# Attention and two MLPs on one core: sums of the second MLP for two blocks at a time on VectorE, shared accumulators, pools that wait by tile

## The chip, the cores and the metric

The kernel runs on one core of one Trainium2 chip. The metric is the device time of one execution in microseconds (us). Before the change it is 1059.33 us, the median of three runs (1056.86 to 1059.69).

## The reference, cut to what matters

All arrays are float32. Attention over 4 batches, 8 heads, 576 positions and 64 columns a head gives a matrix of 2304 tokens by 512. Two MLPs follow; only the second is touched by the change.

```python
def reference(**kwargs):
    attn_out = _attn_ref(...)                      # 4 x 8 x 576 x 64
    x = attn_out.transpose(0, 2, 1, 3).reshape(2304, 512)
    x = _moe_ref(x=x, ...)                         # 512 -> 2048 -> 512, leaky relu
    return _moe2_ref(x=x, ...)

def _moe2_ref(x, w_in, w_out):                     # 512 -> 2048 -> 512
    h = x @ w_in
    r = np.maximum(h, 0.0)
    return ((r * r) @ w_out).astype(np.float32)
```

## The kernel before, in words

The program is written in program order, and a scheduler orders the instructions of each engine by a timeline that it simulates at build time: on each engine an instruction of a later line may be put ahead of one of an earlier line if its operands are there sooner on that timeline. On the chip each engine then keeps the order it was given. All loads and stores go through SyncE's queue (SP), in order as well.

Precision: every float32 operand of a matmul is split into a rounded high part and the rest (`split2`, lines 738 to 741: a cast on ScalarE, line 740, and a subtraction on VectorE, line 741). A product is then three matmuls (`TERMS`: high by high, high by low, low by high).

The first MLP (lines 512 to 722) goes through five chunks of tokens (512, 512, 512, 384, 384), each with 16 steps over the hidden width. Chunk outputs are evacuated to the tiles `xT` (lines 255 and 257) and stored to `xD` in DRAM (line 676), three pieces of 768 tokens. Beside its matmuls the first MLP also prepares the weights of the second (lines 108 to 162). In a step VectorE makes `tt` and `gg` (lines 565, 566) and the low parts of `gs` and `wi` (lines 571, 518).

The second MLP uses Strassen's scheme with seven products for each of its two matrix products, in three passes of 768 tokens (`NPASS`). `part1.close()` (line 727) ends the pools of the first part; the pools `xcp`, `m2` and `ps` (PSUM, eight banks) open in the memory that they leave.

- `load_x` (line 743) loads the pass's inputs in one transfer of 1536 KB into `xl` (line 745). `x_steps` makes the seven split inputs `xc1` to `xc7`: `put` is a split of 128 x 768 elements, `diff` a subtraction in place on GpSimd (line 760). There are seven puts and four diffs.
- `stage1`: for each of eight blocks `q` of the hidden width seven products of six matmuls (line 813), with weights loaded by `w1_group` (line 774, split into `w1h`). Sums of products are made on VectorE (lines 835 to 860); ScalarE applies the relu and GpSimd the square (lines 823, 824). The results of a block are the four parts of a tile `g`, 128 x 4 x 384, one tile for each block.
- `Stage2`: seven sums over the eight blocks in the order of `ORDER2` (products 1, 5, 6, 2, 7, 4, 3), 56 items in all, nine matmuls each (line 927). `prepare` runs `AHEAD` = 3 items ahead: for products 5, 6, 7 and 4 it first subtracts two parts of `g` in place on GpSimd (lines 885, 887, 889, 891), then splits the part into `th` (five buffers). Weights come by `w2_slab` (line 781). Each product has an accumulator of two PSUM banks; when it is done it is copied (ScalarE, line 937) or added (VectorE, lines 940 to 954) to tiles `k`, and two sums of these are made on GpSimd (lines 947, 948). Then `store` writes one quarter of the pass's output.
- `fill` (at the end of the kernel) asks for the next pass's inputs after item 8, and runs one of its eleven x steps at every third item from 16 on.

Of the kernel before, what the change touches and what calls it, by code (L numbers as in the profile page):

```python
# [19 lines left out]
def attention_then_two_mlps(  # L20
# [709 lines left out]
    xcp = ctx.enter_context(tc.tile_pool(name="xcp", bufs=1))  # L730
    m2 = ctx.enter_context(tc.tile_pool(name="m2", bufs=1))
    ps = ctx.enter_context(tc.tile_pool(name="ps", bufs=8, space=PSUM))
# [10 lines left out]
    def load_x(p):  # L743
        xl = xcp.tile([P, NKB, 2 * HT], F32, name="xl", tag="xl")
        nc.sync.dma_start(xl, xD[p])
        xl_now[0] = xl

    def x_steps():


        xl = xl_now[0]
        b11, b12, b21, b22 = (xl[:, 2 * i : 2 * i + 2, j * HT : (j + 1) * HT] for i in range(2) for j in range(2))

        def put(i, src):
            t = xcp.tile([P, 2, 2, HT], F32R, name=f"xc{i}", tag=f"xc{i}")
            split2(t, src)
            xc[i] = t

        def diff(dst, a, b):
            nc.gpsimd.tensor_tensor(dst, a, b, ALU.subtract)  # L760

        return [
            lambda: put(1, b11), lambda: diff(b12, b12, b11), lambda: put(5, b12),
            lambda: diff(b12, b22, b12), lambda: put(6, b12), lambda: diff(b11, b12, b11),
            lambda: put(2, b21), lambda: put(7, b11), lambda: diff(b21, b21, b12),
            lambda: put(4, b21), lambda: put(3, b22),
        ]
# [18 lines left out]
    def stage1(fill):  # L786
# [41 lines left out]
        def begin(q):  # L828
            a, b, c, d = bank("a"), bank("b"), bank("c"), bank("d")
            product(1, q, a, True, True)  # L830
            p1 = t15("p1")
            nc.scalar.copy(p1, a[:, :HT])
            product(6, q, b, True, True)
            u2 = t15("u2")
            nc.vector.tensor_add(u2, p1, b[:, :HT])
            g = m2.tile([P, 4, HT], F32, name="g", tag="g", bufs=NQ)
            g_t[q] = g
            hold[q] = a, b, c, d, p1, u2, g

        def end(q):  # L840
# [3 lines left out]
            act(g[:, 1, :], u2, u2)  # L844

# [22 lines left out]
    AHEAD = 3  # L868

    class Stage2:  # L870
        def __init__(self, p):
            self.p = p
            self.items = [(i, q) for i in ORDER2 for q in range(NQ)]
            self.th, self.slab, self.done = {}, {}, 0

        def prepare(self, n):

            while self.done < min(n, len(self.items)):
                i, q = self.items[self.done]
                self.done += 1  # L880
                if q % 4 == 0:
                    self.slab[i, q // 4] = w2_slab(SLOT[i], q // 4)
                gq = g_t[q]
                if i == 5:
                    nc.gpsimd.tensor_tensor(gq[:, 1], gq[:, 1], gq[:, 0], ALU.subtract)
                elif i == 6:
                    nc.gpsimd.tensor_tensor(gq[:, 1], gq[:, 3], gq[:, 1], ALU.subtract)
                elif i == 7:
                    nc.gpsimd.tensor_tensor(gq[:, 0], gq[:, 1], gq[:, 0], ALU.subtract)
                elif i == 4:  # L890
                    nc.gpsimd.tensor_tensor(gq[:, 2], gq[:, 2], gq[:, 1], ALU.subtract)
                th = m2.tile([P, 2, HT], F32R, name="th", tag="th", bufs=5)
                split2(th, gq[:, PLACE[i]])
# [15 lines left out]
        def run(self, fill):  # L909
# [8 lines left out]

            for n, (i, q) in enumerate(self.items):
                self.prepare(n + AHEAD)  # L920
                if q == 0:
                    acc = (bank("acc0"), bank("acc1"))
                th = self.th.pop((i, q))
                ws = self.slab[i, q // 4]
                for z, (x, y) in enumerate(TERMS):
                    for tb in range(3):
                        nc.tensor.matmul(  # L927
                            acc[tb // 2][:, (tb % 2) * 256 : (tb % 2 + 1) * 256], th[:, x, tb * P : (tb + 1) * P],
                            ws[:, y, q % 4, :], start=(q == 0 and z == 0 and tb != 1),
                            stop=(q == NQ - 1 and z == 2), skip_group_check=True,  # L930
                        )
                fill(n)
                if q < NQ - 1:
                    continue
                if i in (1, 5):
                    d = kept[i] = t3(f"k{i}")
                    both(lambda a, t: nc.scalar.copy(d[:, t], a), acc)
# [3 lines left out]
                elif i == 2:  # L941
                    both(lambda a, t: nc.vector.tensor_add(kept[1][:, t], kept[1][:, t], a), acc)
                    self.store(0, 0, kept[1])
                elif i == 7:
                    kept[3] = t3("k3")
                    both(lambda a, t: nc.vector.tensor_add(kept[3][:, t], kept[2][:, t], a), acc)
                    nc.gpsimd.tensor_tensor(kept[2], kept[2], kept[5], ALU.add)
                    nc.gpsimd.tensor_tensor(kept[5], kept[5], kept[3], ALU.add)
                    self.store(1, 1, kept[5])
                elif i == 4:  # L950
                    both(lambda a, t: nc.vector.tensor_add(kept[3][:, t], kept[3][:, t], a), acc)
                    self.store(1, 0, kept[3])
                else:
# [6 lines left out]
    for p in range(NPASS):  # L960
# [50 lines left out]
```

## Time and profile before

| what | value |
|---|---|
| median of three runs | 1059.33 us |
| the profiled execution's own time | 1059.39 us |
| its span, first to last instruction | 1057.6 us |
| busy: PE / PEld / DVE / ACT / POOL | 93% / 83% / 84% / 58% / 63% |
| mean granted TensorE clock | 0.975 of full speed |

PE is TensorE's matmuls, PEld its weight loads, DVE is VectorE, ACT ScalarE, POOL GpSimd, SP SyncE. A time such as 640.3 is counted from the start of the span. "[13.29 <-ACT xc L740]" behind an instruction says that its engine stood idle for 13.29 us before it and that ScalarE's write of `xc` at line 740 ended the wait. The attention and the first MLP fill the span to 640.3 us, the three passes of the second MLP the rest.

### The profile page before, as it was taken

How to read it: one execution, taken by the hardware profiler on the slowest of the kernel's cores; microseconds unless marked ns; L12 is line 12 of the kernel's file. 1: busy time of each engine (PE TensorE's matmuls, PEld its weight loads, DVE VectorE, ACT ScalarE, POOL GpSimd, SP SyncE). 2: the span in 40 equal slices, each digit the busy share in tenths (PEclk: the TensorE clock that was granted, in tenths of full speed). 3: DMA queues.
4: the chain of work that ended last, by engine and by line, in shares of the span. 5: the costliest groups of instructions: out<-in, count | busy, mean ns of one | idle time of the engine just before them, and what ended most of it. 6: DMA issues, size and time to landing. Idle time of an engine off the chain costs nothing.

```text
span 1057.6 us, 17902 instructions
## 1 busy us (share of the span) xinstructions
PE 987.0 (93%) x6056; PEld 879.0 (83%) x6056; DVE 889.8 (84%) x1575; ACT 613.0 (58%) x1311; POOL 671.6 (63%) x672
## 2 busy tenths in 40 slices
PE   6999999998999999999998994997999987999997
PEld 5777777876667888888987993997799987999997
DVE  8899998889888889888889983899985897858795
ACT  7899998855555446455456542566344663446542
POOL 7788887556454766665665751667933688326881
PEclk9899999999999999999999997998999997999999
DMA  6666654224333345344334527544675444764264
GB/s 172 171 154 170 167 136 104 56 81 139 120 100 134 99 146 180 120 129 149 130 110 144 175 70 285 192 122 142 239 253 183 140 144 144 269 200 130 100 229 130
DMA packets 105611, 160.19 MB, mean 151 GB/s; under 512 B 31760, under 2 KB 80400, under 8 KB 99760
## 3 DMA queue, kind: packets, MB, share of 16 engines
q1 hardware_dynamic: 105520, 159.05, 48.0%
q8 instruction: 48, 0.79, 0.3%
q14 instruction: 43, 0.35, 0.1%
HBM read 118.57 MB, written 31.46 MB: 142 GB/s over the span
## 4 chain that ended last, share of the span: by engine, by line
PE 60%; DVE 27%; issue 4%; ACT 3%; DMA 3%; POOL 2%; SPq 0%; DVEq 0%; ACTq 0%; POOLq 0%
PE acc L927 11%; PE po L663 9%; PE ps_sc L551 7%; DVE th L741 5%; PE a L813 4%; PE b L813 4%; PE c L813 4%; DVE wi_lo L518 4%; PE ps_tr L432 3%; PE ps_xb L482 3%; DVE cv_t L111 3%; PE ph L551 2%; PE ps_xa L471 2%; DVE cv_t L110 2%; DVE tt L565 2%
## 5 line engine op out<-in xcount | busy, mean ns | idle before, releaser
L927 PE MATMUL acc<-w2s,th 128*128 128x256 f32 x1512 | 197.8, 291 | 16.3 <-DVE th L741 13.8
L927 PEld LDWEIGHTS acc<-w2s,th 128*128 128x128 f32 x1512 | 190.6, 197 | 23.0 <-DVE th L741 19.4
L663 PE MATMUL po<-gs,wo_hi 128*128 128x512 f32 (+1 forms) x640 | 189.0, 371 | 5.4 <-DVE gs L571 4.7
L741 DVE TENSOR_TENSOR th<-g,th 128x384 fp32r<-128x384 f32 x168 | 157.6, 982 | 22.3 <-ACT th L740 22.1
L518 POOL TENSOR_TENSOR wo_lo<-wf,wo_hi 128x512 fp32r<-128x512 f32 x80 | 123.0, 1542 | 68.1 <-ACT wo_hi L516 58.0
L551 PE MATMUL ps_sc<-xs,wi_hi 128*128 128x512 f32 (+1 forms) x480 | 139.6, 370 | 3.8 <-DVE xs L536 3.8
L570 ACT CAST gs<-gg 128x512 fp32r<-128x512 f32 (+1 forms) x80 | 46.3, 578 | 166.5 <-DVE gg L566 166.3
L663 PEld LDWEIGHTS po<-gs,wo_hi 128*128 128x128 f32 x640 | 119.0, 189 | 25.6 <-DVE gs L571 9.8
L740 ACT CAST th<-g 128x384 fp32r<-128x384 f32 x168 | 84.4, 513 | 92.1 <-PE acc L927 63.3
L663 PE MATMUL po<-gs,wo_lo 128*128 128x512 f32 (+1 forms) x320 | 117.8, 368 | 0.0
L571 DVE TENSOR_TENSOR gs<-gg,gs 128x512 fp32r<-128x512 f32 (+1 forms) x80 | 76.3, 953 | 32.5 <-ACT gs L570 32.0
L551 PEld LDWEIGHTS ps_sc<-xs,wi_hi 128*128 128x128 f32 x480 | 89.1, 188 | 16.3 <-DVE xs L536 5.0
L400 POOL TENSOR_SCALAR pr<-pr,rs 128x128 f32<-128x128 f32 (+3 forms) x128 | 74.1, 591 | 37.0 <-DVE rs L397 15.6
L741 DVE TENSOR_TENSOR w1h<-w1f,w1h 128x512 fp32r<-128x512 f32 (+1 forms) x96 | 79.7, 841 | 20.0 <-ACT w1h L740 15.2
L551 PE MATMUL ps_sc<-xs,wi_lo 128*128 128x512 f32 (+1 forms) x240 | 89.7, 375 | 7.1 <-DVE wi_lo L518 6.9
L518 DVE TENSOR_TENSOR wi_lo<-wf,wi_hi 128x512 fp32r<-128x512 f32 x80 | 86.0, 1075 | 3.7 <-ACT wi_hi L516 3.6
L114 POOL TENSOR_TENSOR wc<-cv_t,cv_l 128x512 uint32<-128x512 uint32 x32 | 46.2, 1444 | 58.3 <-DVE cv_t L111 21.7
L387 ACT ACTIVATE pr<-pr,nmax 128x128 f32<-128x128 f32 (+3 forms) x128 | 71.0, 559 | 11.6 <-DVE rs L397 5.7
L813 PE MATMUL a<-xc,w1h 128*128 128x384 f32 x288 | 62.9, 344 | 15.3 <-ACT xc L740 13.3
L824 POOL TENSOR_TENSOR g<-u 128x384 f32<-128x384 f32 x48 | 47.4, 989 | 35.3 <-ACT u L823 35.2
L375 DVE CUSTOM_DVE_ANT_0 pr<-ps_sc,mask 128x128 f32<-128x128 f32 (+3 forms) x128 | 60.6, 482 | 10.3 <-PE ps_sc L347 6.5
L663 PEld LDWEIGHTS po<-gs,wo_lo 128*128 128x128 f32 x320 | 60.4, 189 | 7.1
(151 smaller groups left out, 2383.1 us busy)
## 6 DMA issues: line engine op xcount, KB each, us to landing
w2s<-w2D SPq DMA_DIRECT2D x42, 1024.0 KB
w1f<-w1D SPq DMA_DIRECT2D x72, 256.0 KB
raw_w<-in_moe_w_in_dram SPq DMA_DIRECT2D x32, 512.0 KB
w2D<-whl SPq DMA_DIRECT2D x16, 896.0 KB
raw_w<-in_moe_w_out_dram SPq DMA_DIRECT2D x24, 512.0 KB
w1D<-wc SPq DMA_DIRECT2D x8, 896.0 KB
xl<-xD SPq DMA_DIRECT2D x3, 1536.0 KB
QM<-QS SPq DMA_DIRECT2D x15, 288.0 KB
```

What stands on the lines that cost most here:

```text
L375: nc.vector.tensor_tensor_reduce(o, st[u]["S"][h][:, :w], m, -1.0, first, ALU.add, ALU.min, nmax[:, h : h + 1])
L387: last = nc.scalar.activation(o, o, AF.Exp, bias=m, scale=-1.0, accum_out=sums[:, h : h + 1])
L400: nc.gpsimd.tensor_scalar(pr[:, :w], pr[:, :w], rs[:, h : h + 1], 1.0, ALU.mult, ALU.mult)
L518: eng.tensor_sub(lo, w[:, half], hi.bitcast(F32))
L551: nc.tensor.matmul(ph[:, :n], ws[a][:, kb * P : (kb + 1) * P], xs[kb][:, bb, :n], start=(cnt == 0), stop=(cnt == 3 * NKB - 1))
L571: nc.vector.tensor_sub(gs[:, 1, :n], gg[:, :n], gs[:, 0, :n].bitcast(F32))
L663: nc.tensor.matmul(po[m][:, :n], ws[a][:, m * P : (m + 1) * P], gs[:, bb, :n], start=fst, stop=lst)
L740: nc.scalar.copy(dst[:, 0], src)
L741: nc.vector.tensor_sub(dst[:, 1], src, dst[:, 0].bitcast(F32))
L813: nc.tensor.matmul(pt[:, :HT], hl[:, a, c0 + kb * P : c0 + (kb + 1) * P], xc[i][:, b, kb, :], start=(first and cnt == 0), stop=(cnt == 5), ...
L824: nc.gpsimd.tensor_tensor(dst, r, r, ALU.mult)
L927: nc.tensor.matmul(acc[tb // 2][:, (tb % 2) * 256 : (tb % 2 + 1) * 256], th[:, x, tb * P : (tb + 1) * P], ws[:, y, q % 4, :], start=(q == ...
```

## The change

Pools: the three pools of the second MLP are opened with `reuse_waits="tile"`: a tile waits for the tiles whose place it takes, where before it waited for the closed pools as a whole. Inputs: `load_x` loads four quarters in the order in which they are used and makes the seven `xc` tiles there, in a chosen order. Sums: the four diffs of `x_steps` and the subtractions of `g` go from GpSimd to VectorE, and `g`, `th` and the splits hold two blocks; the subtraction of product 5 is made in stage 1. Accumulators: product 2 goes on in the banks of 1, 7 in those of 6, 3 in those of 5; the two GpSimd sums of `k` go, and product 2 is copied where 5 was. The 56 items become 28 of 18 matmuls; the next pass's inputs are asked for after item 4, its x steps run at two of three items from 8 on.

```diff
-    xcp = ctx.enter_context(tc.tile_pool(name="xcp", bufs=1))
-    m2 = ctx.enter_context(tc.tile_pool(name="m2", bufs=1))
-    ps = ctx.enter_context(tc.tile_pool(name="ps", bufs=8, space=PSUM))
+    xcp = ctx.enter_context(tc.tile_pool(name="xcp", bufs=1, reuse_waits="tile"))
+    m2 = ctx.enter_context(tc.tile_pool(name="m2", bufs=1, reuse_waits="tile"))
+    ps = ctx.enter_context(tc.tile_pool(name="ps", bufs=8, space=PSUM, reuse_waits="tile"))
...
     def load_x(p):
         xl = xcp.tile([P, NKB, 2 * HT], F32, name="xl", tag="xl")
-        nc.sync.dma_start(xl, xD[p])
+        for i, j in ((0, 0), (0, 1), (1, 1), (1, 0)):
+            r, c = slice(2 * i, 2 * i + 2), slice(j * HT, (j + 1) * HT)
+            nc.sync.dma_start(xl[:, r, c], xD[p][:, r, c])
         xl_now[0] = xl
+        for i in (1, 5, 6, 3, 2, 7, 4):
+            xc[i] = xcp.tile([P, 2, 2, HT], F32R, name=f"xc{i}", tag=f"xc{i}")
...
         def put(i, src):
-            t = xcp.tile([P, 2, 2, HT], F32R, name=f"xc{i}", tag=f"xc{i}")
-            split2(t, src)
-            xc[i] = t
+            split2(xc[i], src)
 
         def diff(dst, a, b):
-            nc.gpsimd.tensor_tensor(dst, a, b, ALU.subtract)
+            nc.vector.tensor_sub(dst, a, b)
...
-            g = m2.tile([P, 4, HT], F32, name="g", tag="g", bufs=NQ)
-            g_t[q] = g
+            if q % 2 == 0:
+                g_t[q // 2] = m2.tile([P, 2, 4, HT], F32, name="g", tag="g", bufs=NQ // 2)
+            g = g_t[q // 2][:, q % 2]
...
             act(g[:, 1, :], u2, u2)
+            if q % 2:
+                gq = g_t[q // 2]
+                nc.vector.tensor_sub(gq[:, :, 1], gq[:, :, 1], gq[:, :, 0])
...
-    AHEAD = 3
+    AHEAD = 2
...
-            self.items = [(i, q) for i in ORDER2 for q in range(NQ)]
+            self.items = [(i, q) for i in ORDER2 for q in range(NQ // 2)]
...
-                if q % 4 == 0:
-                    self.slab[i, q // 4] = w2_slab(SLOT[i], q // 4)
+                if q % 2 == 0:
+                    self.slab[i, q // 2] = w2_slab(SLOT[i], q // 2)
                 gq = g_t[q]
-                if i == 5:
-                    nc.gpsimd.tensor_tensor(gq[:, 1], gq[:, 1], gq[:, 0], ALU.subtract)
-                elif i == 6:
-                    nc.gpsimd.tensor_tensor(gq[:, 1], gq[:, 3], gq[:, 1], ALU.subtract)
+                if i == 6:
+                    nc.vector.tensor_sub(gq[:, :, 1], gq[:, :, 3], gq[:, :, 1])
                 elif i == 7:
-                    nc.gpsimd.tensor_tensor(gq[:, 0], gq[:, 1], gq[:, 0], ALU.subtract)
+                    nc.vector.tensor_sub(gq[:, :, 0], gq[:, :, 1], gq[:, :, 0])
                 elif i == 4:
-                    nc.gpsimd.tensor_tensor(gq[:, 2], gq[:, 2], gq[:, 1], ALU.subtract)
-                th = m2.tile([P, 2, HT], F32R, name="th", tag="th", bufs=5)
-                split2(th, gq[:, PLACE[i]])
+                    nc.vector.tensor_sub(gq[:, :, 2], gq[:, :, 2], gq[:, :, 1])
+                th = m2.tile([P, 2, 2, HT], F32R, name="th", tag="th", bufs=3)
+                split2(th, gq[:, :, PLACE[i]])
...
-                if q == 0:
-                    acc = (bank("acc0"), bank("acc1"))
+                j = {2: 1, 7: 6, 3: 5}.get(i, i)
+                if q == 0 and i == j:
+                    accs[i] = (bank("acc0"), bank("acc1"))
+                acc = accs[j]
...
-                if i in (1, 5):
-                    d = kept[i] = t3(f"k{i}")
-                    both(lambda a, t: nc.scalar.copy(d[:, t], a), acc)
+                if i == 1:
+                    kept[1] = t3("k1")
+                    both(lambda a, t: nc.scalar.copy(kept[1][:, t], a), acc)
                 elif i == 6:
                     kept[2] = t3("k2")
                     both(lambda a, t: nc.vector.tensor_add(kept[2][:, t], kept[1][:, t], a), acc)
                 elif i == 2:
+                    y = t3("y")
+                    both(lambda a, t: nc.scalar.copy(y[:, t], a), acc)
+                    self.store(0, 0, y)
+                elif i == 7:
                     both(lambda a, t: nc.vector.tensor_add(kept[1][:, t], kept[1][:, t], a), acc)
-                    self.store(0, 0, kept[1])
-                elif i == 7:
-                    kept[3] = t3("k3")
-                    both(lambda a, t: nc.vector.tensor_add(kept[3][:, t], kept[2][:, t], a), acc)
-                    nc.gpsimd.tensor_tensor(kept[2], kept[2], kept[5], ALU.add)
-                    nc.gpsimd.tensor_tensor(kept[5], kept[5], kept[3], ALU.add)
-                    self.store(1, 1, kept[5])
+                    y = t3("y")
+                    both(lambda a, t: nc.vector.tensor_add(y[:, t], kept[1][:, t], a), accs[5])
+                    self.store(1, 1, y)
...
-                if n == 8:
+                if n == 4:
                     load_x(p + 1)
                     steps2.extend(x_steps())
-                if n >= 16 and n % 3 == 0 and steps2:
+                if n >= 8 and n % 3 != 0 and steps2:
                     steps2.pop(0)()
```

## Rows read from the trace of the kernel before

**Rows 1.** The page: busy us of each engine (share of the span) x instructions.

```profile
PE 987.0 (93%) x6056; PEld 879.0 (83%) x6056; DVE 889.8 (84%) x1575; ACT 613.0 (58%) x1311; POOL 671.6 (63%) x672
```

**Rows 2.** Chain that ended last: start, length, engine, tile, line, matmuls.

```profile
980.54 1.04 PE c L813 x6
```

**Rows 3.** Windows, stage 1's matmuls (L813): stretch, length, PE busy, PEld busy, clock, DMA.

```profile
640.30:671.00 30.70, 13.89 (x51) 12.01 (x52) 0.67 0.81 302
720.00:771.00 51.00, 2.40 (x12) 1.79 (x11) 0.93 0.55 196
860.00:891.00 31.00, 1.33 (x6) 1.01 (x6) 0.78 0.39 136
990.00:1022.00 32.00, 1.21 (x6) 1.01 (x6) 1.00 0.60 203
```

**Rows 4.** The same windows, stage 2's matmuls (L927).

```profile
720.00:771.00 51.00, 41.01 (x282) 36.83 (x281) 0.93 0.55 196
860.00:891.00 31.00, 20.56 (x128) 19.61 (x127) 0.78 0.39 136
891.00:930.00 39.00, 39.00 (x328) 39.00 (x327) 1.00 0.80 273
990.00:1022.00 32.00, 30.21 (x242) 29.21 (x241) 1.00 0.60 203
```

**Rows 5.** Timeline from 639.9: SP's issues, then ScalarE's and TensorE's first use.

```profile
639.93 1.81 SPq L676 DMA_DIRECT2D xD<-xT  x4
641.96 1.29 SPq L774 DMA_DIRECT2D w1f<-w1D  x3
643.47 0.32 SPq L745 DMA_DIRECT2D xl<-xD  x1
...
652.84 2.30 ACT L740 CAST xc<-xl 128x768 fp32r<-128x768 f32 x3 [5.15 <-DMA xl<-xD]
...
653.72 0.69 PE L813 MATMUL a<-xc,w1h 128*128 128x384 f32 x1 [13.29 <-ACT xc L740]
```

**Rows 6.** Tile xD (ns, first and last start); SP's timeline, pass 1's load.

```profile
L676 SPq DMA_DIRECT2D xD<-xT x24: 327/408/687, 321.9 to 641.3; - x24
...
667.97 0.32 SPq L745 DMA_DIRECT2D xl<-xD  x1
```

**Rows 7.** Waits, 720:771 us, then 860:891 us: total us, times, longest.

```profile
PE acc L927 <- DVE th L741: 7.2, 7, 3.5
...
ACT th L740 <- POOL g L885: 9.8, 1, 9.8
```

**Rows 8.** Windows, all engines: PE, PEld, DVE, ACT, POOL busy, clock, DMA.

```profile
500.00:640.00 140.00, 132.45 (x738) 128.77 (x737) 121.73 (x163) 71.85 (x130) 84.47 (x64) 0.99 0.37 120
...
730.00:740.00 10.00, 6.59 (x36) 6.12 (x36) 10.00 (x12) 5.35 (x12) 6.79 (x6) 0.66 0.42 143
750.00:760.00 10.00, 9.29 (x65) 8.04 (x65) 10.00 (x8) 3.50 (x8) 10.00 (x8) 1.00 0.57 204
870.00:880.00 10.00, 6.73 (x34) 6.43 (x34) 9.42 (x9) 1.49 (x4) 9.51 (x8) 0.54 0.20 66
```

**Rows 9.** Tiles th, xc, xl and k: ns min/median/max, first and last start.

```profile
L741 DVE TENSOR_TENSOR th<-g,th x168: 543/894/2203, 667.9 to 1046.9; 128x384 fp32r<-128x384 f32 x168
...
L740 ACT CAST xc<-xl x21: 815/827/841, 652.8 to 867.5; 128x768 fp32r<-128x768 f32 x21
L741 DVE TENSOR_TENSOR xc<-xl,xc x21: 945/1290/2414, 653.7 to 872.9; 128x768 fp32r<-128x768 f32 x21
L760 POOL TENSOR_TENSOR xl<-xl x12: 1812/2156/2547, 653.2 to 861.2; 128x768 f32<-128x768 f32 x12
...
L946 DVE TENSOR_TENSOR k<-k,acc x6: 414/548/681, 779.7 to 1035.1; 128x512 f32<-128x512 f32 x3, 128x256 f32<-128x256 f32 x3
```

**Rows 10.** Window 497:612 us: first MLP's matmuls, L551, then L663.

```profile
497.00:612.00 115.00, 60.62 (x305) 53.31 (x305) 0.99 0.42 140
...
497.00:612.00 115.00, 56.36 (x288) 51.28 (x288) 0.99 0.42 140
```

More of the change, by code (lines that the diff above doesn't have):

```diff
@@ L917, in both @@
                 f(acc[1][:, 0:256].rearrange("p (t c) -> p t c", c=256), slice(2, 3))
+            accs = {}
             for n, (i, q) in enumerate(self.items):
                 self.prepare(n + AHEAD)
-                if q == 0:
-                    acc = (bank("acc0"), bank("acc1"))
+                j = {2: 1, 7: 6, 3: 5}.get(i, i)
+                if q == 0 and i == j:
+                    accs[i] = (bank("acc0"), bank("acc1"))
+                acc = accs[j]
                 th = self.th.pop((i, q))
[L924 to L931, printed above, removed]
+                ws = self.slab[i, q // 2]
+                for qq in range(2):
+                    for z, (x, y) in enumerate(TERMS):
+                        for tb in range(3):
+                            nc.tensor.matmul(
+                                acc[tb // 2][:, (tb % 2) * 256 : (tb % 2 + 1) * 256],
+                                th[:, x, qq, tb * P : (tb + 1) * P], ws[:, y, (2 * q + qq) % 4, :],
+                                start=(i == j and q == 0 and qq == 0 and z == 0 and tb != 1),
+                                stop=(q == NQ // 2 - 1 and qq == 1 and z == 2), skip_group_check=True,
+                            )
                 fill(n)
-                if q < NQ - 1:
+                if q < NQ // 2 - 1:
                     continue
-                if i in (1, 5):
-                    d = kept[i] = t3(f"k{i}")
-                    both(lambda a, t: nc.scalar.copy(d[:, t], a), acc)
+                if i == 1:
+                    kept[1] = t3("k1")
+                    both(lambda a, t: nc.scalar.copy(kept[1][:, t], a), acc)
                 elif i == 6:
@@ L941, in run @@
                 elif i == 2:
+                    y = t3("y")
+                    both(lambda a, t: nc.scalar.copy(y[:, t], a), acc)
+                    self.store(0, 0, y)
+                elif i == 7:
                     both(lambda a, t: nc.vector.tensor_add(kept[1][:, t], kept[1][:, t], a), acc)
-                    self.store(0, 0, kept[1])
-                elif i == 7:
-                    kept[3] = t3("k3")
-                    both(lambda a, t: nc.vector.tensor_add(kept[3][:, t], kept[2][:, t], a), acc)
-                    nc.gpsimd.tensor_tensor(kept[2], kept[2], kept[5], ALU.add)
-                    nc.gpsimd.tensor_tensor(kept[5], kept[5], kept[3], ALU.add)
-                    self.store(1, 1, kept[5])
+                    y = t3("y")
+                    both(lambda a, t: nc.vector.tensor_add(y[:, t], kept[1][:, t], a), accs[5])
+                    self.store(1, 1, y)
                 elif i == 4:
-                    both(lambda a, t: nc.vector.tensor_add(kept[3][:, t], kept[3][:, t], a), acc)
-                    self.store(1, 0, kept[3])
-                else:
+                    both(lambda a, t: nc.vector.tensor_add(kept[1][:, t], kept[1][:, t], a), acc)
+                    self.store(1, 0, kept[1])
+                elif i == 3:
                     both(lambda a, t: nc.vector.tensor_add(kept[2][:, t], kept[2][:, t], a), acc)
```

## The prediction, made before the changed kernel ran

> **What bounds the kernel now.** I read the page first: TensorE is busy for 93% of the span [rows 1], so time can only come from stretches in which it idles or runs at a low clock. Next the chain of waits, for TensorE's pace when nothing holds it: six matmuls of stage 1 take 1.04 us, 0.173 us each [rows 2]. The windows give stage 2's pace: 328 matmuls filled a stretch of 39.00 us at full clock, 0.119 us each [rows 4]. With these two prices each stretch of the second MLP shows what it loses, its length less count times price.
>
> - Start, 640.3 to 671: 30.7 us hold 51 matmuls of stage 1 [rows 3], worth 8.8. Lost: 21.9.
> - Pass 0, where stage 2 begins: 51 us hold 12 and 282 [rows 3, 4], worth 2.1 + 33.6. Lost: 15.3.
> - Pass 1, the same place: 31 us hold 6 and 128 [rows 3, 4], worth 1.0 + 15.2. Lost: 14.8.
> - Pass 2, the same place: 32 us hold 6 and 242 [rows 3, 4], worth 1.0 + 28.8. Lost: 2.2.
>
> That is 54.2 us, and 32.3 of it in the last three. The reader is to see in the timeline why the start is lost: the last stores of the first MLP leave at 639.93, the weights are asked for at 641.96 and the inputs at 643.47; they land for ScalarE at 652.84, and TensorE begins after 13.29 idle us [rows 5]. Yet the first pass's tokens come from the first two chunks, and stores to xD began at 321.9 [rows 6]; what the load waited for was the memory of the closed pools. Then the waits: in pass 0 TensorE waits for VectorE's low part of th [rows 7]. In pass 1 ScalarE waited 9.8 us for one subtraction of product 5 on GpSimd [rows 7], queued there behind work for later items. In these stretches VectorE and GpSimd are both full (10.00 of 10 us from 750 to 760, eight instructions each, 1.25 us apiece [rows 8]); the same VectorE instruction takes 0.543 at its fastest [rows 9]. So the two engines hold each other up. Pass 2, which has no next pass to prepare, loses a seventh of the others.
>
> **The change, part by part.** The sum is made on the profiled execution, 1059.39 us, which is the median (1059.33) to 0.1 us.
>
> *Pools that wait by tile, inputs first.* The scheduler does put loads far ahead: pass 1's inputs were asked for at 667.97 [rows 6], in stage 1 of pass 0, though the program asks for them in stage 2. Without the wait for whole pools the quarters of xl, the first weights and the puts can go into the first MLP as their places come free. Only xc3 takes a place that the last chunk uses to its end; its product comes after two others of the next block. Lower bound of the gain: no preparation is moved ahead, but the first quarter lands earlier. The whole load took 652.84 - 643.47 = 9.4 us [rows 5]; at that rate a quarter takes 2.3, and 7.0 are saved. Upper bound: all 21.9. I take 18.9 and leave 3 for hand-overs, as the wait for the inputs is the one that ended last there [rows 5] and it goes altogether. Late next would be xc3, behind the last store.
>
> Splitting the load has a rule against it: the Trainium skill, "SBUF — State Buffer", section "The DMA setup-cost knee", says to put bytes into the largest single transfer, since each pays about 2 us beside its bytes. By its figures, as an estimate, one load of 1536 KB would take 5.6 us and four quarters in series 11.6. The trace measured 9.4 for the one, so the last quarter would come some 2 us later than now: the sum would be 2 us worse if the loads stay behind the first MLP, and the same if they go ahead.
>
> *What goes ahead must be paid for in the first MLP.* Ten of the eleven x steps then lie before 640, each a VectorE instruction of 0.945 to 1.29 us [rows 9]: 9.5 to 12.9 us on VectorE. Up to five weight splits of fewer columns go with them, at most 0.945 each undisturbed: 4.7 more. VectorE from 500 to 640 is busy for 121.73 of 140 us [rows 8]. Their cover is the 18.3 us that are left; without it they lie on the path. From 497 to 612 TensorE already loses 115 - 593 x 0.173 = 12.4 us [rows 10], so VectorE is near the path there; each instruction put ahead of a low part that TensorE waits for costs its length. Bounds: 0 (all in gaps) and 17.6. I take 4, nearer the first, since a gap is where the scheduler puts them. The puts' casts on ScalarE (0.827 each [rows 9]) are covered: ScalarE is busy for 71.85 of these 140 us [rows 8]. On SP some nine loads (four quarters, the first weights) pass the first MLP's last stores and weight loads, at about 0.4 us an issue [rows 5]; SP holds nothing else, and a load that still waits for its place would hold the stores behind it, which only xc3 needs. GpSimd's queue is passed by nothing and loses the diffs.
>
> *Sums of two blocks on VectorE.* A put's subtraction has 768 columns, as a pair's has, and takes 0.945 undisturbed [rows 9]. For three products of stage 2 a pair costs VectorE 2 x 0.945 = 1.89 us, against 18 x 0.119 = 2.14 of TensorE. With nothing on GpSimd but the squares, the pace of 1.25 us a block seen from 750 to 760 (TensorE needs 9 x 0.119 = 1.07) is no more the bound. VectorE in stage 2 of passes 0 and 1: 28 splits x 0.945 = 26.5, 12 subtractions x 0.945 = 11.3, 11 x steps x 0.945 = 10.4, five adds from PSUM in two halves of 0.548 [rows 9] = 5.5; together 53.7 of 504 x 0.119 = 60.0 us of TensorE, 89%. In pass 2, without x steps, 72%. The subtraction of product 5, now four in stage 1 (3.8 us a pass), leaves the queue in which pass 1's 9.8 us arose. Bounds: nothing of the 32.3 is gained, or all. I keep 2.2 in pass 2, as now, and 3.4 in each of the other two, where VectorE is fuller: 9.0 stay, 23.3 go.
>
> *Accumulators, copies, stores.* The two GpSimd sums of k that go were beside TensorE's work; ScalarE's copies and VectorE's adds keep their number. Six banks are held from product 6 to the end of product 2; products 2, 7 and 3 go on in banks last read one or more products before, so no read is waited for. Weight loads and stores keep their counts. Both bounds 0.
>
> Sum: 1059.4 - 18.9 + 4 - 23.3 = 1021.2, say 1021 us.
>
> **The rivals.**
>
> *Nothing goes ahead of the first MLP* (or the tile waits change nothing): only the quarter's 7.0 is gained, the first MLP is not touched: 1059.4 - 7.0 - 23.3 = 1029 us. For it: the scheduler's timeline may see VectorE as full. Against: the early loads [rows 6].
>
> *VectorE becomes the bound of stage 2.* At 89% any misplaced put or weight split, in an order fixed beforehand, holds the next pair: nothing of the 32.3 comes back: 1059.4 - 18.9 + 4 = 1044.5 us. For it: passes 0 and 1 lose seven times what pass 2 loses, and their x steps are now all on VectorE. Against: without GpSimd they are 0.945 and not 2.156 [rows 9].
>
> *Slower: the pair's chain is exposed, and the clock falls.* If VectorE keeps program order, a pair takes subtraction, cast, low part: 0.945 + 0.827 + 0.945 = 2.72 us [rows 9] against 2.14, and TensorE idles in each of 12 pairs a pass. With larger gaps the granted clock was 0.66 and 0.54 of full in two 10 us stretches with TensorE busy for 6.59 and 6.73 [rows 8], between its two levels, 1.2 and 2.4 GHz. At 1.2 GHz a pair takes 4.28, 2.14 more; over 36 pairs 77 us, and the 32.3 would be gone into it: 1059.4 - 18.9 + 4 - 32.3 + 77 = 1089 us. It decides from 47.2 / 2.14 = 22 of the 36 pairs on. Against: gaps as short as those of 750 to 760 left the clock at 1.00 [rows 8].
>
> **How the numbers follow.** About 0.3% is what a measurement of this kernel can tell from no change. The forecast gets 0.67, nothing ahead 0.15, VectorE as the bound 0.12, the falling clock 0.04; 0.02 are left for costs in the first MLP and at the start at their worst ends together, which comes out near no change. The range begins at 1007, where nearly all of the 54.2 is gained and the first MLP pays little, and reaches 1045 to take in the first two rivals. Faster 0.93, within 0.3% 0.03, slower 0.04.
>
> **What would show it.** Right: the loads of xl long before 640, puts among the last chunk's steps, under 5 us idle on TensorE where the second MLP begins, VectorE's th instructions of 768 columns near 0.95 us, GpSimd with squares only after that, passes of some 122 us. Wrong: a gap of 10 us or more at the start; a last chunk longer by over 8 us; TensorE still waiting for th at the beginnings of stage 2 for 10 us a pass; a granted clock near 0.5 in stage 2.

## The result, and the profile after

The changed kernel takes 1043.42 us (median of four runs, 1039.97 to 1044.5), the kernel before 1059.51 beside it (1056.86 to 1059.69). The ratio is 0.9848, with a 95% interval of 0.982 to 0.9877: 16 us faster, inside the range, where 38 were forecast. The profiled execution of after took 1039.97 us (span 1038.2), 3.4 under its median.

The page's busy times, which answer to [rows 1]:

```profile
PE 974.4 (94%) x6056; PEld 872.2 (84%) x6056; DVE 860.0 (83%) x1551; ACT 598.4 (58%) x1227; POOL 523.4 (50%) x558
```

TensorE has the same 6056 matmuls. GpSimd has lost 148 us of work, VectorE 30, though GpSimd's sums came to it as 60 instructions: 84 splits `th` took the place of 168, and one of 768 columns takes about what one of 384 took before [rows 9]. The tile `th` of after, ns min/median/max:

```profile
L741 DVE TENSOR_TENSOR th<-g,th x84: 944/958/1581, 668.6 to 1026.8; 128x768 fp32r<-128x768 f32 x84
```

Where TensorE loses time is read as in the prediction, a stretch's length less its matmuls at 0.173 us (stage 1) and 0.119 us (stage 2). The windows of after, stage 1's matmuls (now line 815), then stage 2's (line 938); columns as in [rows 3]:

```profile
636.40:667.00 30.60, 19.37 (x84) 0.72 0.98 357
710.00:741.00 31.00, 3.62 (x18) 0.89 0.56 185
838.00:884.00 46.00, 4.09 (x22) 0.89 0.48 166
```

```profile
710.00:741.00 31.00, 19.91 (x145) 0.89 0.56 185
741.00:782.00 41.00, 40.99 (x343) 1.00 0.79 272
838.00:884.00 46.00, 34.31 (x254) 0.89 0.48 166
```

| stretch | lost before | lost after |
|---|---|---|
| start of the second MLP | 21.9 | 30.6 - 84 x 0.173 = 16.1 |
| pass 0, where stage 2 begins | 15.3 | 31 - 18 x 0.173 - 145 x 0.119 = 10.6 |
| pass 1, the same place | 14.8 | 46 - 22 x 0.173 - 254 x 0.119 = 12.0 |
| pass 2, the same place | 2.2 | none found |

The rest of the second MLP runs at the two prices (343 x 0.119 = 40.8 of the 41 us from 741 on). So 5.8 us came back at the start and 9.7 in stage 2: together 15.5 of the 16, and under three tenths of the 54.2 that were there to be had. (The expectations below give the start as 5.9, from a window 0.1 us longer with one matmul more in it.)

**The start.** The timeline of after, the rows that answer to [rows 5]:

```profile
635.95 1.80 SPq L676 DMA_DIRECT2D xD<-xT  x4
...
637.84 1.36 SPq L776 DMA_DIRECT2D w1f<-w1D  x3
639.24 1.97 SPq L747 DMA_DIRECT2D xl<-xD  x4
...
645.00 0.83 ACT L740 CAST xc<-xl 128x768 fp32r<-128x768 f32 x1 [1.46 <-DMA xl<-xD]
...
645.89 0.69 PE L815 MATMUL a<-xc,w1h 128*128 128x384 f32 x1 [9.44 <-ACT xc L740]
```

Nothing went ahead. The loads still stand right behind the last stores of the first MLP, as before, and TensorE still idles, for 9.44 us and not 13.29. The first quarter is in use 5.8 us after its issue.

**The beginnings of stage 2.** TensorE's waits from 710 to 741 us, then from 838 to 884 (total, times, longest), for [rows 7]:

```profile
PE acc L938 <- ACT th L740: 6.1, 1, 6.1
...
PE acc L938 <- ACT th L740: 6.9, 1, 6.9
```

One long wait a pass is left. VectorE's timeline in pass 1 shows who made it, and below it ScalarE's and TensorE's rows:

```profile
844.68 2.45 DVE L762 TENSOR_TENSOR xl<-xl 128x768 f32<-128x768 f32 x2
847.05 0.95 DVE L741 TENSOR_TENSOR xc<-xl,xc 128x768 fp32r<-128x768 f32 x1
847.92 0.94 DVE L741 TENSOR_TENSOR th<-g,th 128x768 fp32r<-128x768 f32 x1
848.79 0.54 DVE L864 TENSOR_TENSOR u<-p,b 128x384 f32<-128x384 f32 x1
...
850.72 1.81 DVE L741 TENSOR_TENSOR xc<-xl,xc 128x768 fp32r<-128x768 f32 x2
...
853.33 0.54 DVE L865 TENSOR_TENSOR c<-u,c 128x384 f32<-128x384 f32 x1
...
858.77 1.57 DVE L895 TENSOR_TENSOR g<-g 128x768 f32<-128x768 f32 x1
860.27 0.54 DVE L846 TENSOR_TENSOR u<-u,c 128x384 f32<-128x384 f32 x1
...
862.57 0.95 DVE L895 TENSOR_TENSOR g<-g 128x768 f32<-128x768 f32 x1
863.43 0.94 DVE L850 TENSOR_TENSOR g<-g 128x768 f32<-128x768 f32 x1
```

```profile
864.41 2.31 ACT L740 CAST th<-g 128x768 fp32r<-128x768 f32 x3 [3.05 <-DVE g L850]
```

```profile
865.30 2.08 PE L938 MATMUL acc<-w2s,th 128*128 128x256 f32 x8 [6.95 <-ACT th L740]
```

Lines 864, 865, 846 and 850 are the last block's sums of stage 1, the chain on which the next items of stage 2 depend. TensorE had done `b` by 843.5, yet line 864 starts at 848.79, behind two diffs and a put for the *next* pass; line 846 and line 850 stand behind subtractions for products 6 and 7 (lines 893, 895), which are wanted later. VectorE is never idle from 841 to 864 us. It simply does the wrong things first.

A long wait also costs more than its length, because TensorE's clock is low behind it. All engines' windows of after (columns as in [rows 8]):

```profile
863.00:868.00 5.00, 2.70 (x12) 2.71 (x13) 4.10 (x6) 2.31 (x3) 0.00 (x0) 0.50 0.10 26
868.00:873.00 5.00, 5.00 (x32) 5.00 (x31) 2.67 (x3) 1.30 (x2) 0.00 (x0) 0.68 0.22 52
```

The granted clock is 0.50 of full speed (1.2 of 2.4 GHz) in the first of them and 0.68 in the second. TensorE is busy there for 7.7 us with 44 matmuls that are worth 5.2 at full clock. Of the 12.0 us lost in pass 1 its waits make up 8.4 (6.9, and three short ones of 1.5 together), and 2.5 are this low clock. In pass 0 the low clock behind the wait costs 1.6 of the 10.6 (31 matmuls in 5.33 busy us from 735 to 741, clock 0.74).

### The profile page after: what moved, and what is told of

Read it like the earlier page. It is cut to its first block, busy times and chain, and to the rows that moved or that the text cites. A ratio compares the mean times of both kernels' runs of the same rounds, so it can differ in the third digit from the quotient of the medians.

```text
span 1038.2 us, 17568 instructions
## 1 busy us (share of the span) xinstructions
PE 974.4 (94%) x6056; PEld 872.2 (84%) x6056; DVE 860.0 (83%) x1551; ACT 598.4 (58%) x1227; POOL 523.4 (50%) x558
## 4 chain that ended last, share of the span: by engine, by line
PE 65%; DVE 23%; ACT 4%; issue 4%; DMA 3%; POOL 1%; SPq 1%; DVEq 0%; ACTq 0%; POOLq 0%
PE acc L938 15%; PE po L663 10%; PE ps_sc L551 8%; PE b L815 4%; PE a L815 4%; PE c L815 4%; DVE wi_lo L518 4%; PE ps_tr L432 3%; PE ph L551 2%; PE ps_xb L482 2%; DVE cv_t L111 2%; DVE tt L565 2%; PE ps_xa L471 2%; DVE cv_t L110 2%; PE d L815 2%
## 5 line engine op out<-in xcount | busy, mean ns | idle before, releaser
L938 PE MATMUL acc<-w2s,th 128*128 128x256 f32 x1512 | 189.6, 287 | 16.8 <-ACT th L740 13.0
L938 PEld LDWEIGHTS acc<-w2s,th 128*128 128x128 f32 x1512 | 187.3, 195 | 18.6 <-ACT th L740 13.4
L663 PE MATMUL po<-gs,wo_hi 128*128 128x512 f32 (+1 forms) x640 | 188.0, 369 | 5.1 <-DVE gs L571 4.5
L551 PE MATMUL ps_sc<-xs,wi_hi 128*128 128x512 f32 (+1 forms) x480 | 139.2, 369 | 3.8 <-DVE xs L536 3.8
L663 PEld LDWEIGHTS po<-gs,wo_hi 128*128 128x128 f32 x640 | 118.3, 188 | 24.7 <-DVE gs L571 8.8
L740 ACT CAST th<-g 128x768 fp32r<-128x768 f32 x84 | 69.5, 834 | 84.6 <-PE acc L938 74.3
L663 PE MATMUL po<-gs,wo_lo 128*128 128x512 f32 (+1 forms) x320 | 117.6, 367 | 0.0
L741 DVE TENSOR_TENSOR th<-g,th 128x768 fp32r<-128x768 f32 x84 | 82.1, 982 | 41.3 <-ACT th L740 41.1
L551 PEld LDWEIGHTS ps_sc<-xs,wi_hi 128*128 128x128 f32 x480 | 88.8, 188 | 16.2 <-DVE xs L536 5.0
L826 POOL TENSOR_TENSOR g<-r 128x384 f32<-128x384 f32 x24 | 26.6, 1109 | 149.2 <-ACT r L825 122.0
L571 DVE TENSOR_TENSOR gs<-gg,gs 128x512 fp32r<-128x512 f32 (+1 forms) x80 | 74.1, 926 | 32.5 <-ACT gs L570 32.0
L551 PE MATMUL ps_sc<-xs,wi_lo 128*128 128x512 f32 (+1 forms) x240 | 89.5, 373 | 8.1 <-DVE wi_lo L518 8.0
L518 DVE TENSOR_TENSOR wi_lo<-wf,wi_hi 128x512 fp32r<-128x512 f32 x80 | 83.9, 1048 | 3.7 <-ACT wi_hi L516 3.6
L815 PE MATMUL a<-xc,w1h 128*128 128x384 f32 x288 | 64.0, 344 | 11.1 <-ACT xc L740 9.4
```

The costliest lines, as they stand in the source:

```text
L518: eng.tensor_sub(lo, w[:, half], hi.bitcast(F32))
L551: nc.tensor.matmul(ph[:, :n], ws[a][:, kb * P : (kb + 1) * P], xs[kb][:, bb, :n], start=(cnt == 0), stop=(cnt == 3 * NKB - 1))
L571: nc.vector.tensor_sub(gs[:, 1, :n], gg[:, :n], gs[:, 0, :n].bitcast(F32))
L663: nc.tensor.matmul(po[m][:, :n], ws[a][:, m * P : (m + 1) * P], gs[:, bb, :n], start=fst, stop=lst)
L740: nc.scalar.copy(dst[:, 0], src)
L741: nc.vector.tensor_sub(dst[:, 1], src, dst[:, 0].bitcast(F32))
```

## The experiments

All ran beside the kernel before; its median was between 1058.9 and 1059.6 us in these comparisons. "Under after" means below 1043.42. The third column of the table, the second MLP alone, is the span less the time of the last store's issue of the first MLP (L676), so it leaves out how long the first MLP took, which scatters by some 6 us between profiles of kernels that leave it alone (its last store is issued between 635.95 and 641.75).

| kernel | median, us | second MLP in the profile, us | last store issued at |
|---|---|---|---|
| before | 1059.5 | 417.7 | 639.93 |
| changed | 1043.4 | 402.2 | 635.95 |
| pools wait as a whole | 1043.2 | 402.6 | 637.86 |
| one load | 1044.1 | 404.4 | 640.16 |
| diffs on GpSimd | 1045.9 | 403.6 | 640.45 |
| diffs and subtractions on GpSimd | 1065.6 | 423.7 | 639.60 |
| accumulators alone | 1059.8 | 416.5 | 641.75 |
| subtractions held | 1040.6 | 399.0 | 639.07 |
| x steps held | 1032.4 | 389.2 | 640.69 |
| both held | 1031.4 | 388.5 | 641.03 |
| early input | 1039.7 | 387.0 | 650.40 |
| early input, both held | 1027.4 | 376.5 | 647.70 |
| the same, from step 73 | 1025.4 | 375.9 | 649.26 |
| the same, from step 76 | 1027.0 | 376.2 | 646.81 |

**What holds stage 2 back.** In three kernels the next pass's x steps, the subtractions of products 6 and 7, or both, may not be put ahead of the last subtraction of product 5 on VectorE:

```diff
-                nc.vector.tensor_sub(gq[:, :, 1], gq[:, :, 1], gq[:, :, 0])
+                held[0] = nc.vector.tensor_sub(gq[:, :, 1], gq[:, :, 1], gq[:, :, 0]).ins
...
                 if i == 6:
-                    nc.vector.tensor_sub(gq[:, :, 1], gq[:, :, 3], gq[:, :, 1])
+                    with tc.issue_after(held[0]):
+                        nc.vector.tensor_sub(gq[:, :, 1], gq[:, :, 3], gq[:, :, 1])
...
-                    steps2.pop(0)()
+                    with tc.issue_after(held[0]):
+                        steps2.pop(0)()
```

> The changed kernel with VectorE's subtractions of products 6 and 7 held behind the last subtraction of product 5 of the same pass (same work, another order on VectorE alone). In the changed kernel's trace TensorE idles for 6.07 and 6.95 us in passes 0 and 1 for the last pair of product 5; the add that feeds it starts at 860.27 though its matmuls ended near 857, with five subtractions of products 6 and 7 in between, and the subtraction itself waits about 1 us behind a sixth. Theory A (these subtractions stand in the way): 3 to 4 us come back in each of two passes, 1043.4 to about 1036. Theory B (the next pass's inputs stand in the way, earlier in the chain): under 1.5 us, 1042 to 1044.

> The changed kernel with the x steps of the next pass (VectorE's puts and diffs) held behind the last subtraction of product 5; the subtractions of products 6 and 7 are not held. Theory B: the first sums of the last block start at 848.79 although TensorE's product for them ended near 843.3, behind two diffs, two puts and a low part; without these the chain starts some 4 us earlier and the gaps of 6 to 7 us shrink to 2 or 3: about 1034. Theory A: nothing, 1043. If the held steps then fill VectorE later in stage 2, TensorE waits there and the gain is smaller, down to 0.

> Both holds together. If both kinds of work stand in the way of the same chain, the 10.5 and 11.7 us that passes 0 and 1 still lose go but for 2 to 3 each: 1043.4 - 17 = about 1026. If VectorE is simply full in stage 2 (89% of TensorE's time by the prediction's count), what is moved back stalls TensorE later: 1036 to 1043.

Measured: subtractions held 1040.57 (ratio 0.9826, 0.981 to 0.9842), 2.8 under after; x steps held 1032.37 (0.9743, 0.973 to 0.9756), 11 under; both 1031.37 (0.9733, 0.972 to 0.9747), 12 under. So most of it was the next pass's preparation standing in front of this pass's sums. The 2.8 us are not clear of noise, as the intervals of that kernel and of after overlap. Theory A asked for 6 to 8 us; of the five subtractions that it counts between 857 and 860.27, only three stand there (lines 895, 893, 895), the other two end before. Theory B's 1034 was near, and the 1026 forecast for both holds was missed by 5 us. TensorE's waits with both held, 700 to 930 us:

```profile
PE acc L941 <- DVE th L741: 4.3, 8, 1.0
PE acc L941 <- ACT th L740: 1.8, 6, 0.6
```

No wait is over 1.0 us, where one of 6 to 7 stood in each of the first two passes; the short ones still add up to 6.1 us. VectorE's work is the same: with the x steps held it has 1551 instructions and 861.0 busy us, in after 1551 and 860.0. It is just as dense, too: its timeline in pass 1 with the x steps held shows a line of instructions without a gap, while TensorE runs from 859.23 to 875.23 us without a wait:

```profile
866.05 1.81 DVE L762 TENSOR_TENSOR xl<-xl 128x768 f32<-128x768 f32 x2
867.79 0.94 DVE L741 TENSOR_TENSOR th<-g,th 128x768 fp32r<-128x768 f32 x1
868.66 0.94 DVE L741 TENSOR_TENSOR xc<-xl,xc 128x768 fp32r<-128x768 f32 x1
```

A full VectorE is therefore not what cost the time; the order on it was.

**Off GpSimd, or only in pairs?** The sums in pairs, but on GpSimd as before the change (the subtractions of products 5, 6, 7 and 4 alike):

```diff
-            nc.vector.tensor_sub(dst, a, b)
+            nc.gpsimd.tensor_tensor(dst, a, b, ALU.subtract)
...
-                    nc.vector.tensor_sub(gq[:, :, 1], gq[:, :, 3], gq[:, :, 1])
+                    nc.gpsimd.tensor_tensor(gq[:, :, 1], gq[:, :, 3], gq[:, :, 1], ALU.subtract)
```

> The changed kernel with the input differences and the differences of the hidden blocks back on GpSimd, two blocks at a time as in the changed kernel. Theory: what stage 2 wins comes from leaving GpSimd's long chain; with 768 columns a difference there takes over 2 us, the sums that TensorE waits for are as late as before or later, and the time is 1050 or more. Rival: VectorE's one queue is what holds the rest of the gain back, then taking these sums out of it helps as much as holding them back did, to about 1035.

1065.62 us (1.0065, 1.005 to 1.008), slower than before. Pairs alone bring nothing; the move to VectorE is what the gain needs. Sums of single blocks on VectorE were not run, so what the pairs add there is not shown. The groups of this kernel from 640 to 930 us (busy us, mean ns), first VectorE's, then GpSimd's:

```profile
L741 DVE TENSOR_TENSOR th<-g,th 128x768 fp32r<-128x768 f32 x56 | 81.8, 1480 | 32.0 <-ACT th L740 31.9
...
L741 DVE TENSOR_TENSOR xc<-xl,xc 128x768 fp32r<-128x768 f32 x21 | 31.4, 1511 | 2.9 <-ACT xc L740 2.9
```

```profile
L762 POOL TENSOR_TENSOR xl<-xl 128x768 f32<-128x768 f32 x12 | 27.0, 2257 | 17.1 <-DMA xl<-xD 15.1 <-DVE xc L741 1.9
L897 POOL TENSOR_TENSOR g<-g 128x768 f32<-128x768 f32 x8 | 18.9, 2388 | 6.2 <-DVE th L741 6.2
```

VectorE's split takes 1480 ns on the mean where 944 is the least in after, and a sum costs GpSimd 2.3 us where VectorE needs 0.95. The two engines hold each other up: over the whole run of this kernel the 35 splits `th` during which GpSimd is idle take 0.96 us at most, the 49 that overlap one of its instructions 1.70 on the mean.

**What shortened the start.** Three kernels: the pools opened without the tile waits; one load in place of the four quarters; the four diffs alone on GpSimd (the first line of the diff above).

```diff
-    xcp = ctx.enter_context(tc.tile_pool(name="xcp", bufs=1, reuse_waits="tile"))
+    xcp = ctx.enter_context(tc.tile_pool(name="xcp", bufs=1))
```

```diff
-        for i, j in ((0, 0), (0, 1), (1, 1), (1, 0)):
-            r, c = slice(2 * i, 2 * i + 2), slice(j * HT, (j + 1) * HT)
-            nc.sync.dma_start(xl[:, r, c], xD[p][:, r, c])
+        nc.sync.dma_start(xl, xD[p])
```

> The changed kernel with the three pools waiting for whole pools again. Theory: waiting tile by tile took away waits but moved no work, since the order of the instructions is made as if the pools waited as a whole; the first loads stand behind the last stores of the first MLP either way, so the time stays at that of the changed kernel, 1043 us, within 2. Rival: the waits themselves are where the start of the second MLP won its 5.9 us, then the time is about 1049.

> The changed kernel with the input of a pass in one transfer instead of four quarters. Theory: the quarters are what shortened the start (the first quarter landed 5.8 us after its issue, the whole load of before after 9.4), so one transfer costs about 3.6 us and the time is about 1047. Rival: the start is set by the weights and the queue in front of the load, not by its size, then 1043 stays.

> The changed kernel with the four differences of a pass's input alone back on GpSimd. Theory: the start of the second MLP won most of its 5.9 us by these differences being on VectorE (0.95 us instead of about 1.8 and the way between the engines), so it loses about 4 us; in stage 2 four instructions of 0.95 us leave VectorE's queue in two passes, at most 7.6 us back; together 1040 to 1047. Rival: on GpSimd they run beside VectorE's sums and both slow down, the stalls of stage 2 stay, and the time is about 1050.

Without the tile waits: 1043.2 us (0.9854, 0.9837 to 0.987), no difference. On all five engines its instructions stand in the same order as those of after; only the semaphore waits on the first loads differ. With one load: 1044.13 (0.9859, 0.9841 to 0.9878); the 3.6 us that I expected aren't there, and the times do not tell this kernel from after. With the diffs on GpSimd: 1045.86 (0.9872, 0.9859 to 0.9886), inside what the theory gave. Stage 1's matmuls in the 30.7 us behind the last stores sort it out. The windows, in this order, of one load, of diffs on GpSimd, and of after:

```profile
640.56:671.26 30.70, 16.90 (x71) 0.72 0.92 344
```

```profile
640.85:671.55 30.70, 16.76 (x54) 0.61 0.92 334
```

```profile
636.35:667.05 30.70, 19.42 (x84) 0.72 0.97 356
```

Before has 51 [rows 3]. With the diffs on GpSimd the quarters bring 3 matmuls (51 to 54, 0.5 us), with the diffs on VectorE 13 (71 to 84, 2.2 us). The diffs' move brings 20 with one load (3.5 us) and 30 with quarters (5.2 us). Four more kernels with the start of after (the one without the tile waits and the three with held steps) count 83 to 88 in this stretch, so the 3 are not clear of scatter; the 13 are. The start's gain is the diffs' move first, the quarters a little, the tile waits nothing.

Much of this gain comes by the clock. Behind its idle time TensorE is granted 0.50 of full speed, and in after full speed is back some 5 us sooner than in before or with the diffs on GpSimd. The same 5 us, 21 to 26 us behind the issue of the last stores, in before, with the diffs on GpSimd, and in after (columns as in [rows 3]):

```profile
660.93:665.93 5.00, 3.95 (x12) 3.70 (x12) 0.50 0.54 206
```

```profile
661.45:666.45 5.00, 3.74 (x12) 3.74 (x13) 0.50 0.75 277
```

```profile
656.95:661.95 5.00, 5.00 (x31) 5.00 (x30) 1.00 1.02 384
```

TensorE's waits in this stretch are 13.8 us with the diffs on GpSimd and 11.1 in after. So of the 5.2 us about 2.7 are shorter waits, and the rest goes with the clock that was back sooner.

**Does the start's loss go if work really goes ahead?** The memory is laid out anew, so that the input, its first three parts and stage 1's weights take the places of pools that end before the first MLP does:

```diff
-        xT.append(xpool.tile([P, NKB, CW[c]], F32, name=f"xT{c}"))
+        xT.append((xpool if c < 4 else xpB).tile([P, NKB, CW[c]], F32, name=f"xT{c}"))
...
+    w1p = ctx.enter_context(tc.tile_pool(name="w1p", bufs=1, reuse_waits="tile"))
+    xcB = ctx.enter_context(tc.tile_pool(name="xcB", bufs=1, reuse_waits="tile"))
...
-            xc[i] = xcp.tile([P, 2, 2, HT], F32R, name=f"xc{i}", tag=f"xc{i}")
+            xc[i] = (xcp if i in (1, 5, 6) else xcB).tile([P, 2, 2, HT], F32R, name=f"xc{i}", tag=f"xc{i}")
```

> The changed kernel with its memory laid out so that the inputs of pass 0 (xl, xc1, xc5, xc6) and the first weights of stage 1 take places of pools that end before the first MLP does; the program's lines are otherwise the same. In the changed kernel every engine has the second MLP's work behind all of the first MLP's, as before. Theory C (the order is made as if a new pool waited for whole old ones, and waiting by tile takes only semaphore waits away): now loads, three puts and the first weight splits stand inside the first MLP; the start's loss falls from 16.0 us to about 4, the first MLP pays 0 to 4: about 1031 to 1035. Rival (VectorE has no room in the first MLP): what the start gains the first MLP loses, 1040 to 1045.

> Both remedies at once: the re-laid memory that lets the input, its first three parts and the weights' preparation go ahead into the first MLP, and the next pass's steps and the differences of products 6 and 7 held behind the last block's sums. Theory: the two act in different stages and their gains add (3.7 and 12 us), so about 1027.5 us. Rival: each frees the same VectorE time, then 1031 as with the holding alone.

1039.67 us (0.9808, 0.9794 to 0.9822), and with both holds 1027.4 (0.97, 0.9682 to 0.9718). The first missed the 1031 to 1035 of its theory and lies just under its rival's range; the second came as forecast, so the two gains add. The first shows the trade. SP's and TensorE's timelines of it:

```profile
579.99 0.47 SPq L750 DMA_DIRECT2D xl<-xD  x1
581.94 0.56 SPq L750 DMA_DIRECT2D xl<-xD  x1
...
650.40 1.79 SPq L677 DMA_DIRECT2D xD<-xT  x4
```

```profile
650.73 1.20 PE L818 MATMUL a<-xc,w1h 128*128 128x384 f32 x6
651.77 1.20 PE L818 MATMUL b<-xc,w1h 128*128 128x384 f32 x6
652.81 1.20 PE L818 MATMUL c<-xc,w1h 128*128 128x384 f32 x6
```

Inputs come 70 us before the last store, and TensorE begins stage 1 within 0.4 us of it; the second MLP is 402.2 - 387.0 = 15.2 us shorter, nearly the 16.1 that after lost there. But the last store leaves at 650.40, 9 to 14 us later than in the kernels that leave the first MLP alone. VectorE's groups of this kernel, 500 to 650 us, and the windows 500 to 640 us (columns as in [rows 8], to be held against the same stretch there):

```profile
L744 DVE TENSOR_TENSOR w1h<-w1f,w1h 128x512 fp32r<-128x512 f32 (+1 forms) x5 | 6.9, 1394 | 0.0
...
L765 DVE TENSOR_TENSOR xl<-xl 128x768 f32<-128x768 f32 x3 | 4.2, 1412 | 0.0
L744 DVE TENSOR_TENSOR xc<-xl,xc 128x768 fp32r<-128x768 f32 x3 | 2.8, 946 | 0.0
```

```profile
500.00:640.00 140.00, 124.29 (x685) 117.53 (x684) 130.11 (x169) 74.51 (x133) 86.10 (x63) 1.00 0.46 150
```

13.9 us of VectorE work went ahead. VectorE is busy for 130.1 of the 140 us (121.73 before) and TensorE makes 685 matmuls there where it made 738. Can the price be had for less by placing the work later? Two kernels let the first pass's x steps start only behind step 73 or 76 of the 80 steps of the first MLP:

```diff
+    with tc.issue_after(late[73][0]), tc.issue_after(late[73][1]):
+        for f in x_steps():
+            f()
```

> As the run before, but the input's steps of the first pass may not start on VectorE and ScalarE before step 73 of the 80 of the first MLP, so that they fall into its last 25 us, where VectorE has room. Theory: the 10 us that the first MLP paid came from these steps standing ahead of its own splits on VectorE between 585 and 605 us; moved late, half of it or more comes back: 1017 to 1023. Rival: it was the early transfers on the DMA queues that the first MLP paid for; then about 1027 stays.

> The same with step 76 in place of 73: theory 1016 to 1023, at best 4 us under the other if the steps still delayed splits there; rival 1027. If both are below 1023, the price of going ahead is a matter of where on VectorE it is put.

1025.38 us (0.968, 0.9665 to 0.9696) and 1027.04 (0.97, 0.9686 to 0.9715). Neither fell below 1023: the theory of the place on VectorE fails, or gives 2 us at most. The windows from 580 to 600 and from 620 to 640 us (columns as in [rows 8]), first with early input and both holds, then with the delay to step 73:

```profile
580.00:600.00 20.00, 16.73 (x86) 15.62 (x85) 20.00 (x25) 10.19 (x17) 12.67 (x9) 0.93 0.62 201
620.00:640.00 20.00, 16.81 (x91) 15.43 (x90) 18.22 (x24) 7.95 (x15) 12.36 (x9) 1.00 0.44 139
```

```profile
580.00:600.00 20.00, 19.85 (x115) 19.53 (x114) 19.89 (x26) 11.10 (x20) 11.89 (x9) 1.00 0.70 225
620.00:640.00 20.00, 17.42 (x89) 16.78 (x90) 20.00 (x29) 10.85 (x18) 5.05 (x3) 0.91 0.36 120
```

With both holds and no early input these stretches have 117 and 118 matmuls. Where the x steps were taken away, from 580 to 600, TensorE is back at 115, though the transfers of `xl` are still asked for just then (578.83 to 582.73); where they went, from 620 to 640, it makes 89. From 600 to 620, into which the weight splits moved, it makes 94 and not 116. Over the whole stretch from 500 to 640 us nothing is won: 696 matmuls with VectorE busy for 130.5 us, 688 and 129.5 without the delay. So the price moved along with the VectorE work, and the input's transfers cost nothing that shows. The weights' transfers moved together with their splits, and how the price divides between these two stays open. The version from step 73 is the best that ran, 1025.4 us, 34 us under the kernel before; against the same without the delay, 1027.4, its interval overlaps.

**The accumulators.** The kernel before with products 2, 7 and 3 summed in the banks of 1, 6 and 5 and nothing else:

```diff
-                if q == 0:
-                    acc = (bank("acc0"), bank("acc1"))
+                j = {2: 1, 7: 6, 3: 5}.get(i, i)
+                if q == 0 and i == j:
+                    accs[i] = (bank("acc0"), bank("acc1"))
+                acc = accs[j]
```

> The kernel before with the shared accumulators alone (two products summed in one accumulator, their kept copies and sums gone). Theory: those copies and sums lie beside TensorE's work, so nothing changes: 1059.5 us within 3. Rival: the copies and sums at the ends of the products hold up the engines that the next sums need, then about 1055.

1059.78 us (1.0004, 0.9993 to 1.0015): no change.

## Why the prediction was half right

The direction, the four stretches in which TensorE loses, and most of what could be had (54.2 us) hold: the kernels with early input and held steps show a second MLP of 376 us against 417.7. That is 41 to 42 of the 54 back, of which 32 to 34 are left after what the first MLP pays. The size is wrong, 38 us forecast and 16 measured, because two terms failed. Term by term:

- **Start, 18.9 forecast, 5.8 measured.** The failed step is "Without the wait for whole pools the quarters of xl, the first weights and the puts can go into the first MLP". The tile waits changed which semaphores are waited for, not the order in which instructions stand; the kernel without them has the same order and the same time. I took the early load of pass 1 [rows 6] as a sign that the scheduler would move this one too; but that load's place in memory was already the second MLP's own, while this one's was still the first part's; where the places came from pools that end earlier, the loads did move. So the first rival held for the start, and that its price of 7.0 was near the 5.8 is luck: it put all of it on the quarter landing 7.0 us sooner, and the quarter was in use 5.8 us after its issue, not 2.3, which by itself is worth 0.5 to 2.2 us. The rest is the diffs on VectorE and the clock that is back sooner with them, a gain that I had not put into this term at all.
- **The price in the first MLP, 4 forecast.** Nothing was moved, so nothing was paid. Where it was moved, the second MLP became 15.2 us shorter (early input against after) and 12.0 (388.5 to 376.5, with both holds), and the medians only 3.8 and 4.0: the first MLP paid 11.4 and 8.0. That is inside the bounds of 0 to 17.6, but two to three times the value taken. The row for VectorE from 500 to 640 [rows 8] spoke for the upper half: an engine with 18 free us of 140, on which TensorE waits already, has little cover for 14 us more.
- **Stage 2, 23.3 forecast, 9.7 measured.** VectorE's durations came as said (0.944 at the least, 0.958 the median), GpSimd kept the squares alone, and the 53.7 us of VectorE work counted for stage 2 are near what it does (54.1 from 710 to 782 us, 57.7 from 838 to 918). The failed step is the balance of busy times: "I keep ... 3.4 in each of the other two, where VectorE is fuller". It asks how much VectorE has to do, and not what stands ahead of the one chain that TensorE waits for. With everything on one in-order engine, the x steps and the later subtractions were placed ahead of the last block's sums, and passes 0 and 1 kept one wait of 6 to 7 us each, with a low clock behind it. The second rival named this ("any misplaced put or weight split, in an order fixed beforehand, holds the next pair") but priced it as all or nothing and gave it 0.12; it held for passes 0 and 1 by about 23 of 30 us. That its 1044.5 is so near the 1043.4 measured is luck too: it has 18.9 from the start, 4 paid and nothing from stage 2, and the runs show 5.8, 0 and 9.7. Holding two kinds of steps back gave 12 us, and so showed that the mechanism of the forecast was there to be had.
- **Pass 2**, without next inputs to prepare, lost nothing, where the forecast kept 2.2.
- **Accumulators, 0 forecast**, none measured, in the changed kernel's setting not tried but alone on before.
- **The slower rival** did not come: the granted clock in the two stretches is 0.89, and the waits there are one long and three short ones a pass, not one in every pair. The low clock did come, behind each long wait.
- **The split load.** No loss from splitting can be measured: one load takes 1044.13 us, the quarters 1043.42. The Trainium skill, "SBUF — State Buffer", section "The DMA setup-cost knee", asks for the largest single transfer where transfers are the bound. By its figures four quarters would take 11.6 us, an estimate, some 2 us more than the 9.4 that the trace measured for the one load. These runs don't show that loss. The first part's early arrival may outweigh it; no run separates the two.

## What to carry to other kernels

When sums move from an idle-looking engine to the one that feeds TensorE, count not only its busy share but what stands in its queue ahead of the one chain that TensorE will wait for; work for the next stage is best tied behind that chain by name, which here was worth 12 us in a few lines. A finer wait on reused memory did not by itself move a load here: look whether the order changed. (Whether the re-laid memory needs the finer wait was not tried.) Work sent ahead into an earlier stage, 13.9 us of it on an engine busy for 87% there, cost that stage 8 to 11 us. And a wait of TensorE is to be priced with the low clock behind it, which here added 1.6 and 2.5 us to the two long ones of stage 2.

## What was not expected

The same sum in pairs is slower than before on GpSimd and faster on VectorE, 1065.6 against 1043.4 us: with GpSimd's sums beside it VectorE's 768-column split took 1480 ns on the mean from 640 to 930 us, against 972 in the same stretch of after. The effect was seen before [rows 8, 9], but I had not thought that it would turn the sign.

The Trainium skill, "SBUF — State Buffer", section "SBUF: two separate sides", says that a VectorE instruction with two SBUF inputs and a GpSimd instruction that reads SBUF take one pair of ports in turn, each for its whole length. These rows agree as far as they go: no split took over 2.61 us, less than its own 0.94 and one GpSimd sum of 1.80 (their least lengths) one after the other.
